# Attention backward on one core: dK's and dV's matmul passes and the V^T transposes moved to other places of a hand-written order

## The chip, the cores and the metric

The kernel runs on one core of one Trainium2 chip. The time is device time in microseconds (us) of one execution. The time before is 5152.12 us, the median of three runs (5147.52 to 5171.49).

## The reference

The reference takes the vector-Jacobian product of a block with attention over a cache and a gated linear unit, and returns the forward output and eight gradients. Cut to what matters here:

```python
xn = layernorm(x)                                # x: 2048 x 576, bf16
q = xn @ wq                                      # 32 heads of 128
scores = einsum("bhqd,bhkd->bhqk", q, k_cache) * 128 ** -0.5
p = softmax(scores)                              # 2048 x 2048 for each head
s = einsum("bhqk,bhkd->bhqd", p, v_cache) @ wo
g = silu((sigmoid(xn @ w_gate) * (xn @ w_up)) @ w_down)
out = x + s * g
# and the gradients of A_x, A_k_cache, A_v_cache, A_wq, A_wo, B_w_gate, B_w_up, B_w_down
```

For each head the backward pass needs S = Q K^T again, P = softmax(S), dP = dO V^T, dS = P (dP - delta), and from them dV = P^T dO, dK = dS^T Q, dQ = dS K, and the output O = P V.

## The kernel before, in words

There are three stages: the feed-forward part (up to about 507 us of the profiled execution), the 32 heads of attention (507 to 3757 us), and the weight gradients and dX (the rest). The change lies in the stage of the heads.

A head has 2048 queries in 16 tiles of 128 and 2048 keys in two halves of 1024. Its work is paced by 64 *halves*. Halves 0 to 31 are the S halves: `s_half` (L457) computes a 128 x 1024 block of S with two matmuls (L465) into one of two PSUM buffers (`ps_big`, two banks each), and VectorE scales it and takes the running row minimum (`sneg`, L467). After both halves of a query tile ScalarE does one exponential over 2048 columns (`s_exp`, L476, `Pq`). Halves 32 to 63 are the dP halves: `dp_half` (L486) does two matmuls (L495) into the same two buffers; VectorE makes dS of the second half directly from PSUM (L498), and for most tiles ScalarE first writes `t` for the first half (L501) and VectorE multiplies it (L505).

All other work of a head fills the room between these pairs of matmuls:

- `rows` and `row_mm` (L525): O from the transposed P (`PT`, with `Vn`) and dQ from the transposed dS (`dST`, with `Kn`), 8 matmuls of 128 columns in every half. The transposes are DMA transposes on SyncE's queue (`trans_dma`, L513), except that of dS tile 9, which TensorE makes.
- `kv` and `kv_mm` (L544): dV from `Pq` and `dOn`, then dK from `dSq` and `Qn`. Each has two passes of 128 matmuls, for one half of the keys each. A pass goes through the 16 query tiles in order, eight matmuls for each, and sums in two PSUM accumulators (`acckv`), which ScalarE then copies out to `kv` (`KVE = "ss"`).
- `proj` (L424, L425): Q^T of the next head and dO^T of this one, in four chunks each, copied out by the engines named in `PJE`.
- `pe_transposes` (L431): K^T, V^T, dO and Q in two groups of eight 128 x 128 transposes; a group goes into one bank and is copied out by the engine named ("v" VectorE, "s" ScalarE, L40 or L42).

GpSimd scales `dOn` by the reciprocal row sums (`s_scale`, L484), two query tiles at a time, after the exponentials and VectorE's reciprocals (L480). `o_sink` copies the O rows (`ou`, ScalarE) and VectorE reduces them to `delta` (L578). `dq_sink` scales dQ on VectorE (`dq_n`, L590).

The four remaining PSUM banks (`ps_acc`, tag "acc") are shared, in turn, by the row accumulators, the dK and dV accumulators, the projections and the transposes. Each new tile takes the bank that has been left longest and waits until its last reader has ended.

The order is written by hand. Every piece of work is put in a list by `at(pos, ...)`, where `pos` counts halves from the head's start (`b`); the list is sorted, and TensorE, VectorE and ScalarE execute their shares in exactly that order. So a position is a place in each engine's queue, not a time. The constants are:

- `VA`, `VB`, `KA`, `KB` (L598): first and last position of dV's two passes and dK's two passes; the 128 matmuls of a pass are spread evenly. Positions from 64 on lie among the S halves of the next head.
- `VT_AT`, `DON_AT` (L600): position of the first group of transposes, distance of the second, and the copying engine.
- `PJE` (L599): copying engine of Q^T's and dO^T's chunks.

Of the kernel before, what the change touches and what calls it, by code (L numbers as in the profile page):

```python
# [95 lines left out]
def kernel(  # L96
# [241 lines left out]
    with tc.tile_pool(name="ld2", bufs=2) as ld2, tc.tile_pool(name="ld1q", bufs=1) as ld1q, \  # L338
# [17 lines left out]
        def at(pos, fn, *args):  # L356
            prog.append((pos, len(prog), fn, args))

        def anchor(pos, fn, *args):
            anchors.append((pos, len(anchors), fn, args))  # L360
# [169 lines left out]
        def rows(pos, step, width, hs, T, rhs, g, sinks):  # L530
            bx = Box()
            sink, after = sinks
            for j in range(GQ):
                for kt in range(NT):
                    at(pos + step * j + width * kt / NT, row_mm, bx, hs, T, rhs, g * GQ + j, kt, sink)
            if after:
                at(pos + step * (GQ - 1) + width + AFTER, after)
# [11 lines left out]
        def kv(pos, end, hs, slabs, rhs, half, out_dram):  # L549
            ov = out_dram.rearrange("(p t) d -> p t d", t=NT)  # L550
            bx = Box()
            bx.acc = [None, None]

            def sink(acc, i):
                c = half * 2 + i
                kv_t = stg.tile([P, KPC, P], bf, name="kv")
                alt.copy(kv_t[:], acc[:], eng=KVE[i])
                nc.gpsimd.dma_start(ov[:, c * KPC:(c + 1) * KPC, :], kv_t[:])

            n = 2 * KPC  # L560
            for qt in range(NT):
                for j in range(n):
                    at(pos + (end - pos) * (qt * n + j) / (NT * n), kv_mm, bx, hs, slabs, rhs, half, qt, j, sink)

        def o_sink(hs, g):
            gs = slice(g * GQ, (g + 1) * GQ)
            bx = Box()

            def sink(acc):
                bx.ou = wt.tile([P, GQ, P], bf, name="ou")  # L570
                alt.copy(bx.ou[:], acc[:], eng=OUE)
                bx.prod = wt.tile([P, GQ, P], f32, name="prod", bufs=1)
                nc.gpsimd.tensor_tensor(bx.prod[:], bx.ou[:], hs.dOn[:, gs, :], op=ALU.mult)

            def after():
                prod, ou = bx.prod, bx.ou
                o_n = stg.tile([P, GQ, P], bf, name="o_n", bufs=1)
                nc.vector.tensor_reduce(hs.delta[:, gs], prod[:], axis=AX.X, op=ALU.add)  # L578
                nc.gpsimd.tensor_scalar(hs.negdelta[:, gs], hs.delta[:, gs], -1.0, None, op0=ALU.mult)  # L579
                nc.gpsimd.tensor_tensor(o_n[:], ou[:], bcast(hs.rinv_all[:, gs], GQ), op=ALU.mult)  # L580
                nc.gpsimd.dma_start(on2_d[g * CH:(g + 1) * CH, hs.h * P:(hs.h + 1) * P].rearrange("(t p) d -> p t d", p=P), o_n[:])

            return sink, after

        def dq_sink(hs, g):
            gs = slice(g * GQ, (g + 1) * GQ)

            def sink(acc):
                dq_n = stg.tile([P, GQ, P], bf, name="dq_n")
                nc.vector.tensor_tensor(dq_n[:], acc[:], bcast(hs.rsc[:, gs], GQ), op=ALU.mult)  # L590
                nc.gpsimd.dma_start(dq2_d[g * CH:(g + 1) * CH, hs.h * P:(hs.h + 1) * P].rearrange("(t p) d -> p t d", p=P), dq_n[:])  # L591

            return sink, None
# [1 line left out]
        H1 = 2 * NT  # L595
        HEAD = 2 * H1
        XO, XQ = 12.1, 12.1
        VA, VB, KA, KB = (22, 38.0), (38.5, 53.5), (58.0, 69.5), (70.5, 82.0)  # L598
        QP, DO, KVE, PJE, OUE = (41.0, 3.0), (4.0, 2.5), "ss", "sv", "s"  # L599
        KT_AT, DON_AT, VT_AT, QN_AT = (46.3, 2, "v"), (7.2, 5, "v"), (22.2, 2, "v"), (38.3, 2, "s")  # L600
        EXP_AT, RINV_AT, PT_AT, DST_AT, AFTER = 2.1, 4.6, 2.7, 2.0, 3.5
        WO_AT = 50.0
        MAN = {mybir.EngineType.PE, mybir.EngineType.DVE, mybir.EngineType.Activation}
        for h in range(H):
            hs = Head(h)
            b = h * HEAD
            back = lambda x: b - HEAD + x if h else b - 14 + x / 8
            at(back(35.0), load_w, hs)
            at(back(35.1), load_kv, hs)
            for c in range(NCH):  # L610
                at(back(QP[0] + QP[1] * c), proj, hs, "QT", c, PJE[0])
                at(b + DO[0] + DO[1] * c, proj, hs, "dOT", c, PJE[1])
            at(b + DO[0] - 2, prep_wo, hs, "s")
            for g in range(2):
                at(back(KT_AT[0] + KT_AT[1] * g), prep_kt, hs, g, KT_AT[2])
                at(b + DON_AT[0] + DON_AT[1] * g, prep_don, hs, g, DON_AT[2])
                at(b + VT_AT[0] + VT_AT[1] * g, prep_vt, hs, g, VT_AT[2])
                at(b + QN_AT[0] + QN_AT[1] * g, prep_qn, hs, g, QN_AT[2])
            for p in range(NT // 2):
                at(b + 4 * p + 2 + RINV_AT, s_rinv, hs, p)  # L620
                at(b + max(4 * p + 2.1 + RINV_AT, DON_AT[0] + DON_AT[1] * (p // 4) + 0.5), s_scale, hs, p)
            for qt in range(NT):
                p1, p2 = b + 2 * qt, b + H1 + 2 * qt
                for hf in range(NHF):
                    anchor(p1 + hf, s_half, hs, qt, hf)
                    anchor(p2 + hf, dp_half, hs, qt, hf)
                at(p1 + EXP_AT, s_exp, hs, qt)
                if qt in PE_P:
                    for g in range(2):
                        at(p1 + 5.3 + g, trans_pe, hs.PT, hs.P, qt, "PT", g, "s")  # L630
                else:
                    at(p1 + PT_AT, trans_dma, hs.PT, hs.P, qt, "PT")
                if qt in PE_DS:
                    for g in range(2):
                        at(p2 + 4.3 + g, trans_pe, hs.dST, hs.dS, qt, "dST", g, "sv"[g])
                else:
                    at(p2 + DST_AT, trans_dma, hs.dST, hs.dS, qt, "dST")
            for g in range(NG):
                rows(b + 8 * g + XO, 2, 2, hs, hs.PT, "Vn", g, o_sink(hs, g))
                rows(b + H1 + 8 * g + XQ, 2, 2, hs, hs.dST, "Kn", g, dq_sink(hs, g))  # L640
            for half, (pv, pk_) in enumerate(((VA, KA), (VB, KB))):
                kv(b + pv[0], b + pv[1], hs, hs.P, "dOn", half, out_3[0, h])
                kv(b + pk_[0], b + pk_[1], hs, hs.dS, "Qn", half, out_2[0, h])
# [380 lines left out]
```

## Time and profile before

| | us |
|---|---|
| median of three runs | 5152.12 |
| profiled execution | 5157.5 |
| its span (first to last instruction) | 5155.7 |
| stage of the 32 heads | about 3250 |
| one head, median of its length | 100.3 |
| TensorE busy in the span | 4983.8 |
| VectorE busy | 3231.5 |
| ScalarE busy | 2285.3 |

The span of the profiled execution is the time from the first to the last instruction; its own time of 5157.5 us includes 1.8 us around that. In the profile PE is TensorE's matmuls, PEld its weight loads, DVE is VectorE, ACT is ScalarE, POOL is GpSimd, SP is SyncE. `out<-in` names what an instruction writes and reads, and L467 is line 467 of the kernel. Matmuls overlap in the records: a matmul of 128 columns is listed with 0.22 us, but they follow each other every 0.0556 us. The granted TensorE clock is 1.00 throughout the heads.

### The profile page before, as it was taken

To read this page: it belongs to the slowest core of one execution; us is meant where nothing else is said; L and a number is where in the kernel's file an instruction comes from. 1 tells how busy PE (TensorE), PEld (TensorE's weight loads), DVE (VectorE), ACT (ScalarE), POOL (GpSimd) and SP (SyncE) were. 2 spreads that over 40 slices of the span, in tenths; PEclk is the share of its full clock that TensorE was granted. 3 is DMA by queue.
4 is the path that set the end of the run, shared out by engine and by line. 5 is a ranking of instruction groups with operands and counts; after the bars stand their busy time and mean duration, and the time that the engine had idled before them with its cause. 6 is when DMAs were issued, how large, how long until landed. Compare 5 with 4: busy or idle time off the path is not lost.

```text
span 5155.7 us, 124622 instructions
## 1 busy us (share of the span) xinstructions
PE 4983.8 (97%) x53232; PEld 3490.9 (68%) x54160; DVE 3231.5 (63%) x5070; ACT 2285.3 (44%) x2878; POOL 1388.1 (27%) x1981
## 2 busy tenths in 40 slices
PE   8999999999999999999999999999899999999999
PEld 3444777777777777777777777777655555554554
DVE  5545888888888888888888888888733222210101
ACT  6531665566556556655655665566501222100000
POOL 2222333233223323332332333233222222111000
PEclk9999999999999999999999999999999999999999
DMA  7478999999999999999999999999999776697775
GB/s 281 184 210 166 189 191 196 195 199 195 196 196 196 197 201 199 196 202 196 199 196 198 199 197 195 199 199 195 205 200 246 209 209 196 199 246 166 158 153 118
DMA packets 2710509, 1013.89 MB, mean 197 GB/s; under 512 B 2523360, under 2 KB 2643936, under 8 KB 2709952
## 3 DMA queue, kind: packets, MB, share of 16 engines
q1 hardware_dynamic: 2628256, 726.57, 81.9%
q0 software_dynamic: 81696, 279.29, 18.5%
q8 instruction: 423, 6.93, 0.5%
q14 instruction: 134, 1.10, 0.1%
HBM read 172.54 MB, written 201.00 MB: 72 GB/s over the span
## 4 chain that ended last, share of the span: by engine, by line
PE 84%; DVE 6%; DMA 5%; issue 4%; SPq 1%; ACT 0%; DVEq 0%; ACTq 0%; another core or an unknown queue 0%
PE acckv L544 17%; PE acc L525 14%; PE acc L965 8%; PE dp L495 6%; PE sp L465 5%; DVE sneg L467 5%; PE accp L424 5%; PE accw L848 5%; DMA dST<-dSq 3%; PE g_ps L249 3%; PE u_ps L252 3%; PE accd L833 3%; PE acc L306 3%; PE acc L903 2%; PE dh L782 2%
## 5 line engine op out<-in xcount | busy, mean ns | idle before, releaser
L476 ACT ACTIVATE Pq<-sneg,nm 128x2048 bf16<-128x2048 bf16 x512 | 1024.5, 2001 | 389.5 <-DVE sneg L467 386.4
L525 PE MATMUL acc<-Kn,dST 128*128 128x128 bf16 x8192 | 1066.6, 219 | 28.1 <-DMA dST<-dSq 26.1
L544 PE MATMUL acckv<-dOn,Pq 128*128 128x128 bf16 x8192 | 1032.1, 219 | 15.4 <-POOL negdelta L579 0.2
L525 PE MATMUL acc<-Vn,PT 128*128 128x128 bf16 x8192 | 1023.2, 219 | 10.9 <-DMA PT<-Pq 9.1
L498 DVE SCALAR_TENSOR_TENSOR dSq<-dp,delta,Pq 128x1024 bf16<-128x1024 f32 x608 | 773.9, 1281 | 351.6 <-PE dp L495 249.7
L544 PE MATMUL acckv<-Qn,dSq 128*128 128x128 bf16 x8192 | 897.7, 220 | 8.4 <-issue 0.2
L544 PEld LDWEIGHTS <-Pq 128*128 128x128 bf16 x8192 | 793.8, 98 | 117.6 <-issue 0.9
L525 PEld LDWEIGHTS <-dST 128*128 128x128 bf16 x8192 | 758.8, 98 | 162.9 <-DMA dST<-dSq 34.1
L525 PEld LDWEIGHTS <-PT 128*128 128x128 bf16 x8192 | 766.4, 98 | 151.2 <-DMA PT<-Pq 11.3
L544 PEld LDWEIGHTS <-dSq 128*128 128x128 bf16 x8192 | 719.7, 98 | 99.8 <-issue 0.3
L467 DVE TENSOR_SCALAR_CACHE_REDUCE sneg<-sp,nm 128x1024 bf16<-128x1024 f32 x512 | 656.5, 1282 | 83.8 <-PE sp L465 46.4
L467 DVE TENSOR_SCALAR_CACHE_REDUCE sneg<-sp 128x1024 bf16<-128x1024 f32 x512 | 625.1, 1221 | 60.4 <-PE sp L465 42.0
L501 ACT ACTIVATE t<-dp,negdelta 128x1024 bf16<-128x1024 f32 x416 | 463.6, 1114 | 425.7 <-PE acc L525 233.2
L465 PE MATMUL sp<-KT,QT 128*128 128x512 bf16 x1763 | 548.4, 380 | 33.0 <-DVE sneg L467 26.1
L495 PE MATMUL dp<-VT,dOT 128*128 128x512 bf16 x1728 | 540.4, 379 | 0.8 <-DVE dSq L498 0.8
L484 POOL TENSOR_TENSOR dOn<-dOn,rinv_all 128x256 bf16<-128x256 bf16 x256 | 155.9, 609 | 657.7 <-DVE rinv_all L480 540.6
L505 DVE TENSOR_TENSOR dSq<-t,Pq 128x1024 bf16<-128x1024 bf16 x416 | 319.5, 768 | 0.0
L848 PE MATMUL accw<-dd_blk,xn_all 128*128 128x512 bf16 x1134 | 250.6, 379 | 0.9
L978 DVE SCALAR_TENSOR_TENSOR junk<-dxn,xn_all 128x576 f32<-128x576 f32 x16 | 12.1, 758 | 368.2 <-ACT dxn L973 368.2
L965 PEld LDWEIGHTS <-cf 128*128 128x128 bf16 x2304 | 145.7, 98 | 142.7 <-DMA cf<-dg_d 4.5
L591 POOL DMA_DIRECT2D dq_d<-dq_n x128 | 98.7, 771 | 459.5 <-DVE dq_n L590 450.9
L848 PEld LDWEIGHTS <-xn_all 128*128 128x128 bf16 x1152 | 111.4, 98 | 133.8
(182 smaller groups left out, 6694.3 us busy)
## 6 DMA issues: line engine op xcount, KB each, us to landing
out_dram<-kv POOLq DMA_DIRECT2D x256, 128.0 KB, 5.2
h_d<-h_row POOLq DMA_DIRECT2D x48, 384.0 KB, 2.7
a_d<-a_row POOLq DMA_DIRECT2D x48, 384.0 KB, 2.6
b_d<-b_row POOLq DMA_DIRECT2D x48, 384.0 KB, 3.2
a_blk<-a_d SPq DMA_DIRECT2D x18, 1024.0 KB, 5.6
b_blk<-b_d SPq DMA_DIRECT2D x18, 1024.0 KB, 20.8
du_d<-dd_blk POOLq DMA_DIRECT2D x18, 1024.0 KB, 8.5
dg_d<-dd_blk POOLq DMA_DIRECT2D x18, 1024.0 KB, 11.5
```

The lines of the kernel that those rows point to most:

```text
L424: nc.tensor.matmul(acc[:], lhsT=w[:, i, :], rhs=srcT[:, i, cs], start=(i == 0), stop=False)
L465: nc.tensor.matmul(sp[:, c * CH:(c + 1) * CH], lhsT=hs.QT[:, qs], rhs=hs.KT[:, hf * HW_ + c * CH: hf * HW_ + (c + 1) * CH], start=True, st ...
L467: nc.vector.tensor_scalar(sneg[:, hf * HW_:(hf + 1) * HW_], sp[:], -SCALE, None if hf == 0 else nm[:, hf - 1:hf], op0=ALU.mult, op1=ALU.mi ...
L476: nc.scalar.activation(Pq[:], sneg[:], AF.Exp, bias=nm[:, hf:hf + 1], scale=-1.0, accum_out=hs.rs_all[:, qt:qt + 1])
L495: nc.tensor.matmul(dp[:, c * CH:(c + 1) * CH], lhsT=hs.dOT[:, qs], rhs=hs.VT[:, hf * HW_ + c * CH: hf * HW_ + (c + 1) * CH], start=True, s ...
L498: nc.vector.scalar_tensor_tensor(dSq[:, hsl], dp[:], hs.delta[:, qt:qt + 1], Pq[:, hsl], op0=ALU.subtract, op1=ALU.mult)
L501: nc.scalar.activation(t[:], dp[:], AF.Identity, bias=hs.negdelta[:, qt:qt + 1], scale=1.0)
L505: nc.vector.tensor_tensor(dSq[:, hsl], t[:], Pq[:, hsl], op=ALU.mult)
L525: nc.tensor.matmul(bx.acc[:, j, :], lhsT=T[qt][:, kt, :], rhs=getattr(hs, rhs)[:, kt, :], start=(kt == 0), stop=(kt == NT - 1))
L544: nc.tensor.matmul(bx.acc[i][:, jj, :], lhsT=slabs[qt][:, k0:k0 + P], rhs=getattr(hs, rhs)[:, qt, :], start=(qt == 0 and jj == 0), stop=(q ...
L848: nc.tensor.matmul(acc[:], lhsT=xn_all[:, st, i * P:(i + 1) * P], rhs=dd_blk[:, st, :, :], start=(st == 0), stop=(st == NT - 1))
L965: nc.tensor.matmul(accs[sl][j][:, :nn], lhsT=ch[:, kk, sl * P:(sl + 1) * P], rhs=w_[:, n0:n0 + nn], start=(pi == 0 and kk == 0), stop=(las ...
```

## The change

Three lines of constants and the two places that read one of them are changed. dV's first pass begins 0.7 halves earlier and ends 0.6 earlier, its second is spread over 16.1 instead of 15 halves. dK's first pass begins 1.5 halves later and ends 1.1 later, its second begins 0.6 later and ends 2.9 later, at 84.9, which is half 20.9 of the next head. The second group of dO's transposes comes one half later. V^T's two groups stand at 22.6 and 26.6 instead of 22.2 and 24.2, and ScalarE copies them. The third chunk of dO^T is copied by ScalarE instead of VectorE. The number of instructions on each engine's path is otherwise the same.

```diff
-        VA, VB, KA, KB = (22, 38.0), (38.5, 53.5), (58.0, 69.5), (70.5, 82.0)
-        QP, DO, KVE, PJE, OUE = (41.0, 3.0), (4.0, 2.5), "ss", "sv", "s"
-        KT_AT, DON_AT, VT_AT, QN_AT = (46.3, 2, "v"), (7.2, 5, "v"), (22.2, 2, "v"), (38.3, 2, "s")
+        VA, VB, KA, KB = (21.3, 37.4), (37.9, 54.0), (59.5, 70.6), (71.1, 84.9)
+        QP, DO, KVE, PJE, OUE = (41.0, 3.0), (4.0, 2.5), "ss", ("ssss", "vvsv"), "s"
+        KT_AT, DON_AT, VT_AT, QN_AT = (46.3, 2, "v"), (7.2, 6, "v"), (22.6, 4, "s"), (38.3, 2, "s")
...
-                at(back(QP[0] + QP[1] * c), proj, hs, "QT", c, PJE[0])
-                at(b + DO[0] + DO[1] * c, proj, hs, "dOT", c, PJE[1])
+                at(back(QP[0] + QP[1] * c), proj, hs, "QT", c, PJE[0][c])
+                at(b + DO[0] + DO[1] * c, proj, hs, "dOT", c, PJE[1][c])
```

## The prediction

> **What bounds the kernel now.** I read the page first (engine shares, chain), then the chain of waits in one head, then the timelines of ScalarE and VectorE there.
>
> ```profile
> PE 4983.8 (97%) x53232; PEld 3490.9 (68%) x54160; DVE 3231.5 (63%) x5070; ACT 2285.3 (44%) x2878; POOL 1388.1 (27%) x1981
> PE 84%; DVE 6%; DMA 5%; issue 4%; SPq 1%; ACT 0%; DVEq 0%; ACTq 0%; another core or an unknown queue 0%
> ```
>
> TensorE is the bound: only what leaves it idle in a head can be won, 32 times over. The chain, in order of time (start, length, what), shows where VectorE takes it from TensorE:
>
> ```profile
> 2457.85 0.45 PE sp L465 x2
> 2458.34 0.07 issue
> 2458.41 1.23 DVE sneg L467 x2
> 2459.64 0.09 DVE rinv_all L480
> 2459.77 0.58 DVE sneg L467
> 2460.35 0.63 issue
> 2460.98 1.24 DVE sneg L467 x3
> ...
> 2464.77 0.06 DVE VT L42
> ...
> 2470.09 0.09 DVE sneg L467
> 2470.23 0.38 PE sp L465
> ```
>
> Numbering a head's halves 0 to 63 (S halves 0 to 31, dP halves from 32), 2457.6 is the start of half 18 of this head. From the starts of the weight loads of L465 and L495 a head takes 100.3 us (median). Its TensorE work, from the same chain, is 0.43 for a half's two 512-column matmuls, 0.0556 for each 128-column matmul (0.45 for eight) and 1.08 for a projection: 97.9 us. Half by half, length minus work is almost everywhere 0.00 to 0.01 us. The exceptions:
>
> - half 12: 0.39. The second transpose group of dO^T wants the bank that dq_n (L590) still empties.
> - halves 20, 21, 22: 0.25, 0.54, 0.27. Halves 18 to 21 hold 0.88 us of matmuls, while VectorE's two sneg take 2.56 per pair (2458.41 to 2460.98).
> - half 27: 0.46. VectorE is still behind by two V^T copies and one delta.
> - half 41: 0.16 (a Qn copy), half 58: 0.09 (the t of half 56).
>
> Together 2.16 us a head. Some heads lose 1 to 2 us more at halves 56 to 60, where dST arrives late.
>
> **The change, part by part.** The built order shows that nothing is added or removed on TensorE; 289 matmuls of dK and dV in the S halves replace 269. Halves 18 to 21 go from 0.88 to 1.38, 1.38, 1.32 and 1.21 us, V^T's groups go from halves 22 and 24 to 22 and 26, dO^T's second group from 12 to 13; halves 58 and 59 fall from 1.54 and 1.49 to 0.88 and 1.21.
>
> *Gains.* Halves 20 to 22: the work now exceeds VectorE's 1.28 a half, so 1.06 goes. Half 27: VectorE loses two copies of 0.69, so 0.46 goes; the delta left at half 23 delays sneg by 0.6, inside the lead of two score buffers. Half 12: dq_n ended 1.0 after the half's start (2448.84 against 2447.84); the group now starts 1.9 after it, so 0.39 goes. Sum 1.91. The dO^T copy (0.69 on VectorE, 0.585 as ScalarE's QT row) hides behind half 10 on either engine.
>
> *Costs.* Each stretch of dK or dV needs two of the four accumulator banks, and ScalarE empties the old ones between softmax exponentials of 2.0 us:
>
> ```profile
> 2457.48 1.07 ACT L40 CAST kv<-acckv 128x512 bf16<-128x512 f32 x2 [0.22 <-ACT Pq L476]
> 2458.44 2.02 ACT L476 ACTIVATE Pq<-sneg,nm 128x2048 bf16<-128x2048 bf16 x1
> 2460.34 0.20 ACT L476 ACTIVATION_READ_ACCUMULATOR Pq<-sneg,nm 128x1 f32 x1
> 2460.43 0.58 ACT L40 CAST ou<-acc 128x512 bf16<-128x512 f32 x1
> 2461.09 2.00 ACT L476 ACTIVATE Pq<-sneg,nm 128x2048 bf16<-128x2048 bf16 x1
> ```
>
> Before, dK's last copies had four halves before dV wanted the banks. Now dK ends at 20.9 and dV starts at 21.3; ScalarE's order there becomes exp 8, ou, exp 9, the two dK copies, exp 10. The build makes dV's second accumulator (half 21, eleventh filler) wait for the first dK copy.
>
> *Half 21.* Count from half 17's start. Halves 17 to 20 take 1.44, 1.38, 1.39, 1.32, so half 20 starts at 4.21 and half 21 at 5.53. ou starts 0.31 after half 20 (as 2482.40 against a half start of 2482.09) and holds ScalarE 0.49: until 5.01. exp 9 could go at 4.83, so ou ends last; it runs to 7.00. First dK copy: 7.00 to 7.58 (0.58); TensorE follows an ending copy by 0.05 (2490.10 to 2490.15). The matmul could have run at 5.53 + 0.06 + 0.43 + 10 x 0.0556 = 6.58. Wait 1.05. Behind it in TensorE's queue stands half 22, so all stands.
>
> *Half 28.* The dK copies end ScalarE's work at 7.95, exp 10 at 9.94, V^T copy 1 (1.0, as the Qn copy's 1.018) at 10.94. Half 22 starts at 7.85, half 24 at 10.95; delta puts its sneg at 12.11 and the next at 13.46, so exp 12 runs from 14.79 to 16.78 and V^T copy 2 to 17.80. Half 28 starts at 16.70; its new row accumulator takes that bank and could start at 17.25: wait 0.60. Nothing waits for V^T itself so early, only for the bank.
>
> *Half 7.* dK's first half ends at 6.6, so exp 2 is now ahead of its copies. From half 5: exp 2 from 2.02 to 4.01, copy to 4.59; the second half's first matmul could start at 4.39: wait 0.25.
>
> *Half 59.* Half 58 without dK lasts 0.88; half 59 needs the buffer that VectorE reads from 2516.62 to 2517.90. It could start 0.88 after 2516.76, at 2517.64: wait 0.31. dST of tile 8 is reached 0.5 us sooner; its landing had 1.2 us to spare (median), so nothing more in most heads.
>
> *Half 35.* dV's tile 14 moves from half 36 to 35.4; POOL's scaling ends 4.74 after half 32 and the matmul could start at 4.76: 0.05.
>
> *Elsewhere.* 0.16 and 0.09 stay; half 40 is one matmul shorter and its Qn group one matmul later: 0.11 more at half 41. exp 15 starts 1.76 after half 32 as before (2478.55), so PT transposes on SP keep their lead of 2 to 9 us. POOL stores dK one to three halves later, in time it had idle.
>
> The Trainium skill, "PSUM — Partial Sum Buffer", section "Engine vs sequencer instructions", says that ScalarE's queue is a strict FIFO: a copy can't pass an exponential. The first row above, a copy released by the end of an exponential, agrees; if a copy could pass, the wait at half 21 would be nothing.
>
> The Trainium skill, "ScalarE: Activation LUTs", section "Rules for kernel authors", sends simple elementwise work to VectorE as up to three times faster in bf16, which speaks against moving the V^T copies. The rows say 1.018 against 0.686 us; kept on VectorE they would cost the 0.46 of half 27 and save the 0.60 of half 28, 4 us less in all.
>
> **The sum.** After: 0.25 + 1.05 + 0.60 + 0.05 + 0.27 + 0.09 + 0.31 = 2.62 us a head; before 2.16. The 0.46 more, times 31, is 14 us. Head 0 has no dK ahead of it and gains about 1.5 (an estimate from 1.06 + 0.46); behind the last head 15 more matmuls stand alone, 0.8 us. Net 14 us. The profiled execution was 5157.5 us (span 5155.7), 5.4 above the median 5152.1; I add to the median: 5166. What this measurement can tell from no change is about 0.5%, 26 us or 0.8 us a head.
>
> **Rivals.** *The fillers work (faster).* ScalarE is free in time at halves 21 and 28: 1.05 and 0.60 vanish, 1.19 us a head is won, 37 us: 5115. For: ScalarE is busy only 44%. Against: its order, and 2.0 us exponentials just ahead of the copies. It decides if the first dK copy ends by 6.5 on the scale above.
>
> *dST arrives late (slower).* With dK gone from halves 58 and 59, tile 8's rows lose 0.5 us of cover. For, from the view of waits (us, times, longest):
>
> ```profile
> PE acc L525 <- DMA dST<-dSq: 26.1, 24, 6.5
> ```
>
> In 8 of 32 heads tile 8 landed with no time to spare. Against: the median has 1.2 us to spare. If landings come 0.7 later, from transposes running closer together, 0.8 us a head is added on top of the forecast: 14 + 25, 5191. From a landing 0.7 us later than now it decides.
>
> *The change doesn't do what it says*: the built order has the matmuls in halves 18 to 21, so no.
>
> **How the numbers follow.** Forecast 0.53, faster rival 0.17, slower 0.30. The forecast's own range is 5140 to 5182 (half 28 between 0 and 1.2, half 21 between 0.8 and 1.3, half 59 between 0 and 0.5 us). Of its 0.53, 0.48 lies within 0.5% and 0.05 above; 0.02 of the slower rival stays within, and 0.01 of the faster one. So faster 0.16, same 0.51, slower 0.33. The range reaches to both rivals: 5112 to 5195.
>
> **What would show it.** Right: in TensorE's waits a new group, acckv L544 or the halves behind it held by ScalarE's kv copies at half 21, about 1 us in every head; no idle at halves 12, 20 and 27; a head of about 100.8 us. V^T rows on ScalarE with about 1.02 us each, exp 12 ahead of the second. Wrong: halves 21 and 28 at their matmul time (then the faster rival), or dST in the waits at half 60 well above 26 us (the slower one).

## The result: 0.4% slower, and the profile after

The changed kernel takes 5179.42 us (median of 21 runs, 5164.31 to 5206.34); the kernel before, run beside it, 5161.39 (21 runs, 5144.1 to 5193.11). The ratio is 1.0037, with a 95% interval of 1.0023 to 1.0051: 18 us slower by the medians, 19 by the ratio. Forecast were 5166 against 5152.12, 14 us slower. Its profiled execution took 5182.66 us, its span 5180.8.

The page of the changed kernel, engine shares and chain:

```profile
PE 4979.2 (96%) x53263; PEld 3493.4 (67%) x54160; DVE 3187.1 (62%) x4974; ACT 2349.9 (45%) x2974; POOL 1386.3 (27%) x1981
PE 82%; DMA 5%; DVE 5%; issue 4%; ACT 4%; SPq 0%; ACTq 0%; DVEq 0%; another core or an unknown queue 0%
```

TensorE's share of the chain falls from 84 to 82%. ScalarE, at 0% before, now has 4% of it. TensorE's waits in the changed kernel (us in total, times, longest) say where:

```profile
PE acckv L544 <- ACT kv L40: 32.7, 62, 0.9
PE acc L525 <- DMA dST<-dSq: 31.6, 20, 5.1
PE acc L525 <- ACT VT L40: 13.3, 30, 0.6
...
PE sp L465 <- DVE sneg L467: 7.9, 12, 1.8
...
PE dp L495 <- DVE dSq L498: 3.8, 20, 0.9
```

The first and third rows are new: the dK and dV accumulators wait for ScalarE's copies twice in each of 31 heads, and the rows of O wait for the V^T copy once in each of 30. In exchange, the waits for VectorE's sneg have fallen from 26.1 us to 7.9, and those of the dO^T group for dq_n are gone. The chain of the changed kernel, in the same head as before, shows halves 21 and 28 (start, length, what):

```profile
2471.55 0.39 ACT Pq L476
2472.02 1.09 issue
2473.11 0.19 ACT Pq L476
2473.30 0.48 ACT kv L40
2473.82 0.22 PE acckv L544
...
2480.93 2.09 ACT Pq L476 x2
2483.03 0.91 ACT VT L40
2483.98 0.22 PE acc L525
```

Both times the chain runs through an exponential, the copy queued behind it on ScalarE, and the matmul that wanted the bank. (Its "issue" of 1.09 lies inside the exponential, as the timeline of ScalarE there shows.)

```profile
2471.20 2.00 ACT L476 ACTIVATE Pq<-sneg,nm 128x2048 bf16<-128x2048 bf16 x1
2473.11 0.19 ACT L476 ACTIVATION_READ_ACCUMULATOR Pq<-sneg,nm 128x1 f32 x1
2473.20 1.06 ACT L40 CAST kv<-acckv 128x512 bf16<-128x512 f32 x2
```

Two lengths of a head are used from here on, both from the starts of the weight loads, with heads counted from 0. The *mean head* is the mean length of heads 1 to 30: 101.87 us against 100.97 before the change. The *undisturbed head* takes for each of the 64 halves the median of its length over heads 2 to 30 and adds these up: 100.91 us against 100.32. Waits that come in less than half of the heads are in the first and not in the second. The idle time of TensorE by half, median, in us:

| half | 7 | 12 | 20 | 21 | 22 | 27 | 28 | 35 | 41 | 58 | 59 | 62 |
|---|---|---|---|---|---|---|---|---|---|---|---|---|
| before | 0.01 | 0.39 | 0.25 | 0.54 | 0.27 | 0.46 | 0 | 0 | 0.16 | 0.09 | 0.01 | 0 |
| forecast | 0.25 | 0 | 0 | 1.05 | 0 | 0 | 0.60 | 0.05 | 0.27 | 0.09 | 0.31 | 0 |
| after | 0.39 | 0 | 0 | 0.99 | 0.01 | 0 | 0.60 | 0.05 | 0.22 | 0.09 | 0.32 | 0.11 |

### The profile page after: what moved, and what is told of

Its sections match the earlier page's. It is cut to its first block, busy times and chain, and to the rows that moved or that the text cites. A ratio compares the mean times of both kernels' runs of the same rounds, so it can differ in the third digit from the quotient of the medians.

```text
span 5180.8 us, 124624 instructions
## 1 busy us (share of the span) xinstructions
PE 4979.2 (96%) x53263; PEld 3493.4 (67%) x54160; DVE 3187.1 (62%) x4974; ACT 2349.9 (45%) x2974; POOL 1386.3 (27%) x1981
## 3 DMA queue, kind: packets, MB, share of 16 engines
q14 instruction: 133, 1.09, 0.1%
## 4 chain that ended last, share of the span: by engine, by line
PE 82%; DMA 5%; DVE 5%; issue 4%; ACT 4%; SPq 0%; ACTq 0%; DVEq 0%; another core or an unknown queue 0%
PE acckv L544 16%; PE acc L525 14%; PE acc L965 7%; PE dp L495 6%; PE sp L465 5%; PE accw L848 5%; PE accp L424 4%; DVE sneg L467 3%; PE u_ps L252 3%; PE g_ps L249 3%; PE accd L833 3%; PE acc L306 3%; DMA dST<-dSq 3%; PE acct L431 3%; PE acc L903 2%
## 5 line engine op out<-in xcount | busy, mean ns | idle before, releaser
L544 PE MATMUL acckv<-dOn,Pq 128*128 128x128 bf16 x8192 | 1066.5, 219 | 34.3 <-ACT kv L40 25.7
L525 PE MATMUL acc<-Kn,dST 128*128 128x128 bf16 x8192 | 1052.9, 220 | 34.9 <-DMA dST<-dSq 31.6
L525 PE MATMUL acc<-Vn,PT 128*128 128x128 bf16 x8192 | 1049.5, 219 | 23.2 <-ACT VT L40 13.3
L498 DVE SCALAR_TENSOR_TENSOR dSq<-dp,delta,Pq 128x1024 bf16<-128x1024 f32 x608 | 773.9, 1281 | 347.5 <-PE dp L495 320.4
L544 PE MATMUL acckv<-Qn,dSq 128*128 128x128 bf16 x8192 | 923.0, 220 | 18.6 <-ACT kv L40 7.0
L525 PEld LDWEIGHTS <-PT 128*128 128x128 bf16 x8192 | 791.6, 98 | 165.0 <-issue 29.8
L544 PEld LDWEIGHTS <-dSq 128*128 128x128 bf16 x8192 | 732.3, 98 | 99.6 <-issue 0.6
L591 POOL DMA_DIRECT2D dq_d<-dq_n x128 | 98.6, 771 | 446.2 <-DVE dq_n L590 433.4
```

The costliest lines, as they stand in the source:

```text
L498: nc.vector.scalar_tensor_tensor(dSq[:, hsl], dp[:], hs.delta[:, qt:qt + 1], Pq[:, hsl], op0=ALU.subtract, op1=ALU.mult)
L525: nc.tensor.matmul(bx.acc[:, j, :], lhsT=T[qt][:, kt, :], rhs=getattr(hs, rhs)[:, kt, :], start=(kt == 0), stop=(kt == NT - 1))
L544: nc.tensor.matmul(bx.acc[i][:, jj, :], lhsT=slabs[qt][:, k0:k0 + P], rhs=getattr(hs, rhs)[:, qt, :], start=(qt == 0 and jj == 0), stop=(q ...
```

## Experiments

Two theories about the time stood against each other. **A**, the one that the prediction's sum rests on: a head lasts as long as TensorE's matmuls and its regular waits, so each wait taken away is won 31 times. **B**: the 31 DMA transposes of a head are already near what their queue can do, and TensorE time that is won comes back as waits for them. The table has all kernels; "DMA" is the number of transposes that a head sends to the DMA queue, "waits" is TensorE's waits for dST and PT together, and a ratio is to the kernel before on the same chip. Of the waits, 13 to 23 us lie in the last head of every kernel (20.9 of the 35.2 before, 13.9 of the 39.6 after). The undisturbed and the mean head come from the one profiled execution of each kernel; the expectations below say "median head" for the undisturbed one. The plain median of the heads' lengths is another number, for it contains the irregular waits: 100.8 us in f_all_banks_free, 103.4 and 103.7 in the two kernels with 32.

| kernel | DMA | undisturbed head | mean head | waits | ratio to before, 95% interval |
|---|---|---|---|---|---|
| before | 31 | 100.32 | 100.97 | 35.2 | 1 |
| after | 31 | 100.91 | 101.87 | 39.6 | 1.0037 [1.0023, 1.0051] |
| e_copies_before_exp9 | 31 | 100.24 | 101.18 | 45.4 | 1.0031 [1.0008, 1.0053] |
| e_vt_by_vector | 31 | 100.32 | 101.05 | 38.8 | 1.0036 [1.0015, 1.0057] |
| e_dk_first_back | 31 | 100.22 | 102.16 | 67.6 | 1.004 [1.0019, 1.006] |
| e_before_don6 | 31 | 99.95 | 101.39 | 51.6 | 0.9991 [0.9971, 1.0011] |
| f_all_banks_free | 31 | 99.34 | 101.21 | 66.0 | 1.0003 [0.9987, 1.0018] |
| f_all_tile7_pe | 31 | 99.62 | 101.60 | 73.3 | 1.0028 [1.0012, 1.0045] |
| f_after_tile7_pe | 31 | 101.17 | 101.70 | 34.4 | 1.0041 [1.0023, 1.0059] |
| f_before_don6_tile7_pe | 31 | 100.10 | 101.16 | 40.7 | 0.9992 [0.9976, 1.0009] |
| g_before_no_pe_tile | 32 | 100.61 | 103.81 | 117.4 | 1.018 [1.0156, 1.0204] |
| g_all_no_pe_tile | 32 | 99.33 | 103.90 | 161.5 | 1.0187 [1.0165, 1.0209] |
| g_all_pt14_pe | 30 | 100.89 | 100.91 | 12.8 | 0.998 [0.9965, 0.9995] |
| i_all_ds10_pe | 30 | 99.84 | 100.23 | 22.8 | 0.9929 [0.9904, 0.9954] |

### One term at a time

**Half 21: dK's end in front of exponential 9** (the changed kernel, with dK's second pass 0.9 halves shorter):

```diff
-        VA, VB, KA, KB = (21.3, 37.4), (37.9, 54.0), (59.5, 70.6), (71.1, 84.9)
+        VA, VB, KA, KB = (21.3, 37.4), (37.9, 54.0), (59.5, 70.6), (71.1, 84.0)
```

> The changed kernel, with dK's second pass ending at 84.0 instead of 84.9, so that ScalarE's two dK copies come before exp 9 in its order; dV still begins at 21.3. Theory (the bank waits behind one exponential): the idle of half 21 falls from 0.99 to 0.1 us or less, half 28 keeps about 0.6, a head takes 100.0 instead of 100.9 us, the kernel is about 28 us faster than the changed one (0.5%). Rival (ScalarE has too much to do between halves 18 and 28, whatever the order): the wait of half 21 is only moved, halves 28 and 35 grow by what 21 loses, a head stays at 100.6 us or more.

Half 21's idle went from 0.99 to 0.00, half 28's from 0.60 to 0.85, and the undisturbed head to 100.24. The wait at half 21 is therefore the copy behind that exponential. The time did not follow: it stayed 0.3% over before, where 28 us less than the changed kernel were expected.

**Half 28: the V^T copies on VectorE again**, still four halves apart:

```diff
-... VT_AT, QN_AT = ... (22.6, 4, "s"), (38.3, 2, "s")
+... VT_AT, QN_AT = ... (22.6, 4, "v"), (38.3, 2, "s")
```

> The changed kernel, with V^T's copies by VectorE again, at the new places 22.6 and 26.6. Theory (half 28 waits for the bank of ScalarE's second V^T copy): half 28 falls from 0.60 to nearly nothing, VectorE's lag gives 0.05 to 0.25 us at halves 25 to 28, 0.35 us a head or 11 us in all is won. Rival (VectorE then lags as in the kernel before): 0.46 us or more of idle appears at halves 25 to 28, and 4 us or nothing is won.

Half 28's 0.60 went, and half 27 stayed at 0.00: with four halves between them, VectorE carries both copies without falling behind at half 27, at least as long as half 21 still waits its 0.99. The prediction had charged 0.46 for that. The undisturbed head is before's again, 100.32, and still the ratio is 1.0036. (The profiled execution of this kernel, 5163 us, was the fastest of its 12; their median is 5184. So its mean head of 101.05 is too short for a typical one.)

**Halves 7, 59 and 62: dK's first pass where it was:**

```diff
-        ... (59.5, 70.6), (71.1, 84.9)
+        ... (58.0, 69.5), (71.1, 84.9)
```

> The changed kernel, with dK's first pass at 58.0 to 69.5 as before (the second stays at 71.1 to 84.9). Theory (ScalarE's copies behind exp 2 cost half 7, the uncovered halves 58 and 59 cost 59, 60 and 62): 0.39, 0.32 and 0.11 go, and the mean of half 60 falls from 0.36 to about 0.16: 0.8 us a head in the median, 1.0 in the mean, 25 to 31 us in all. Rival (the later dST landings come from the whole order's closer spacing, not from these halves): half 60 keeps its mean of 0.36, and about 0.8 us a head are won.

The three waits went and the undisturbed head fell by 0.69 us, but the mean rose to 102.16: waits for dST are 52.2 us and for PT 15.4, where the changed kernel had 31.6 and 8.0.

**Half 12: only dO^T's second group one half later**, in the kernel before:

```diff
-        ... DON_AT ... = (7.2, 5, "v")
+        ... DON_AT ... = (7.2, 6, "v")
```

> The kernel before, with the second group of dO^T's transposes one half later (13.2 instead of 12.2), nothing else. Theory: only half 12's 0.39 us goes, a head takes 99.9 instead of 100.3 us, 12 us less than before (0.24%). Rival (the stall moves to half 13 or to the O rows that start there): no change.

Half 12's 0.39 went and the undisturbed head fell by 0.37, while the waits for DMA rose by 16 us. No difference in time can be told.

### The waits for ScalarE's copies away at once, and another tile for TensorE

**The waits of halves 7, 21, 28, 59 and 62 taken away** (the changed kernel, with dV's first pass and both of dK's moved, and V^T on VectorE):

```diff
-        VA, VB, KA, KB = (21.3, 37.4), (37.9, 54.0), (59.5, 70.6), (71.1, 84.9)
+        VA, VB, KA, KB = (20.9, 37.4), (37.9, 54.0), (58.0, 69.5), (70.5, 84.0)
...
-... VT_AT, QN_AT = ... (22.6, 4, "s"), (38.3, 2, "s")
+... VT_AT, QN_AT = ... (22.6, 4, "v"), (38.3, 2, "s")
```

> The changed kernel with every wait that its profile shows taken away by its place: dV from 20.9, dK's first pass back at 58.0 to 69.5, the second at 70.5 to 84.0 (its copies ahead of exp 9), V^T's copies by VectorE at 22.6 and 26.6. Theory A (the waits of halves 7, 21, 28 and 59 are what the change lost): a median head of about 98.6 us with 0.5 us of idle, and the time follows: 1.7 us a head or about 50 us less than the kernel before (1%). Theory B (the transposes by DMA land too late for a shorter head): the median head is 98.6 us as well, but TensorE's waits for dST and PT grow from 35 us by 20 to 50 us, and the kernel wins less than 0.5% or nothing.

The undisturbed head is 99.34, 1.57 less than in the changed kernel and 0.98 less than before. It did not come down to the expected 98.6: half 26 has a new wait of 0.34 for VectorE's sneg, behind the first V^T copy and a delta, half 58 waits 0.40, mostly for dST, and halves 41 and 35 keep 0.22 and 0.16. By A 0.98 us a head is 30 us faster than before; measured is 1.0003. Its waits:

```profile
PE acc L525 <- DMA dST<-dSq: 47.6, 37, 5.6
PE acc L525 <- DMA PT<-Pq: 18.4, 20, 5.7
PE sp L465 <- DVE sneg L467: 11.3, 40, 1.0
```

The gain is there in an undisturbed head and is taken back in irregular waits for the transposes. Half 58, where dST is waited for most, is where TensorE begins the rows of tile 7, and half 60 where it begins those of tile 8. Three kernels gave TensorE dS's tile 7 in place of tile 9:

```diff
-    PE_DS = {9}
+    PE_DS = {7}
...
-                        at(p2 + 4.3 + g, trans_pe, hs.dST, hs.dS, qt, "dST", g, "sv"[g])
+                        at(p2 + 7.3 + 2 * g, trans_pe, hs.dST, hs.dS, qt, "dST", g, "sv"[g])
```

In f_all_banks_free:

> The kernel of the run before, with dS tile 7 transposed by TensorE in place of tile 9 (at 53.3 and 55.3), so that tile 9 goes by DMA, where the built order leaves it ten halves. Nothing else: the same number of transposes by each. Theory B: the waits for dST at half 58 vanish and those at 60 shrink, 0.4 to 0.8 us a head or 12 to 25 us less than the run before. Theory A: no difference (within 0.2%).

In the changed kernel:

> The changed kernel, with dS tile 7 transposed by TensorE in place of tile 9. Theory B: the mean excess of half 58 (0.31 us over the median head) goes, half 60 keeps part of its 0.34; 10 to 15 us less than the changed kernel, while halves 7, 21 and 28 keep 0.39, 0.99 and 0.60. Theory A: no difference.

In e_before_don6:

> The kernel before, with the second dO^T group one half later and dS tile 7 transposed by TensorE in place of tile 9. Theory B: half 12's 0.39 and half 58's mean of 0.4 to 0.7 us are gone, 0.8 us a head or 25 us less than the kernel before (0.5%). Theory A: 12 us less (0.24%).

Half 58's mean idle fell to 0.07 us in all three, and half 60's below 0.1, so the lateness of tiles 7 and 8 can be cured there. The time that B expected from it, 10 to 25 us, did not come; the lateness comes back elsewhere. The waits of f_all_tile7_pe:

```profile
PE acc L525 <- DMA PT<-Pq: 48.0, 50, 3.8
PE acc L525 <- DMA dST<-dSq: 25.3, 19, 6.7
```

Together they are 7.3 us more than without the move: dST's have halved, and P's late tiles at halves 34 and 36 have taken their place. None of the three became faster.

### Changing the number of DMA transposes

**One more in the kernel before** (32 by DMA, 0.89 us less on TensorE):

```diff
-    PE_DS = {9}
+    PE_DS = set()
```

> The kernel before, with dS's tile 9 transposed by the DMA queue like the other fifteen, so that 32 transposes a head go by DMA and none by TensorE; TensorE's matmuls of a head fall from 97.86 to 96.97 us. Theory A (TensorE's work and its regular waits set the time of a head): 0.89 us less on each of 31 heads, 28 us or 0.5% faster than before. Theory B (the DMA queue's transposes, 31 to a head, are near their limit, and time won on TensorE comes back as waits for them): TensorE's waits for DMA, some 35 us in the trace of before, grow by 28 us or more; the time is the kernel before's within 0.3%, or longer.

**The same in f_all_banks_free:**

> The kernel of f_all_banks_free, with dS's tile 9 transposed by DMA too: 32 transposes a head by DMA. Theory A: a median head of 98.5 us and 28 us faster than f_all_banks_free. Theory B: the median head falls, but the mean head stays between 101 and 102.5 us, TensorE's waits for DMA pass 90 us, and the time is f_all_banks_free's or longer.

Both are 1.8 to 1.9% slower than before, with less work on TensorE: A had the sign wrong. B had the sign but not the size: it expected "within 0.3%, or longer", and heads of up to 102.5 us where 103.8 and 103.9 were found. The waits of g_before_no_pe_tile:

```profile
PE acc L525 <- DMA dST<-dSq: 80.4, 61, 5.9
PE acc L525 <- DMA PT<-Pq: 37.0, 47, 3.1
```

Two kernels whose undisturbed heads differ by 1.28 us have mean heads within 0.1 us of each other. Divided by 32, 103.81 and 103.90 give 3.24 and 3.25 us for one transpose: here the DMA transposes, one after another, and not TensorE, set the head. Times 31 that is 100.6 us, and no kernel with 31 transposes in the table has a mean head below 100.97.

**One fewer**, f_all_banks_free with P's tile 14 by TensorE and VectorE:

```diff
-    PE_P = set()
+    PE_P = {14}
...
-                        at(p1 + 5.3 + g, trans_pe, hs.PT, hs.P, qt, "PT", g, "s")
+                        at(p1 + 5.3 + g, trans_pe, hs.PT, hs.P, qt, "PT", g, "v")
```

> The kernel of f_all_banks_free, with P's tile 14 transposed by TensorE and copied by VectorE, so that 30 transposes a head go by DMA and two tiles by TensorE; TensorE's matmuls of a head grow by some 0.9 us. Theory A: 31 x 0.9 = 28 us slower than f_all_banks_free, a median head of 100.2 us. Theory B: TensorE's waits for DMA, 66 us in f_all_banks_free, fall by half or more, and the mean head comes to within 0.7 us of the median head; the time is f_all_banks_free's within 0.3% or shorter.

Mean and undisturbed head are the same to 0.02 us. In heads 0 to 30 no wait for DMA remains; the two below lie in the last head:

```profile
PE acct L431 <- DVE PT L42: 18.5, 32, 0.6
PE sp L465 <- DVE sneg L467: 11.2, 42, 1.0
...
PE acc L525 <- DMA dST<-dSq: 7.0, 1, 7.0
...
PE acc L525 <- DMA PT<-Pq: 5.8, 1, 5.8
```

TensorE has 0.89 us more work a head than in f_all_banks_free, and a new wait of 0.6 for VectorE's copy, and the kernel is not slower for it (0.998 against 1.0003). The undisturbed head is 0.7 us above the 100.2 of A's sum, most of it that new wait; the mean, which sets the time, is below f_all_banks_free's.

**One fewer, in a better place**: dS's tile 10 instead, in halves 56 and 57, where a half has only 0.88 us of work:

```diff
-    PE_DS = {9}
+    PE_DS = {9, 10}
```

> The kernel of f_all_banks_free, with dS's tile 10 transposed by TensorE beside its tile 9 (halves 56 and 57, where a half is shortest and two acc banks are free), so that 30 transposes a head go by DMA and P's all do. Theory B, with the limit read from the two kernels of 32 transposes (103.8 us a head, 3.24 us for each): 30 transposes need 97.3 us, below TensorE's own time, so the mean head comes down to the median, that is 99.34 us + 0.89 us of transposes, less 0.3 us of half 58's wait: 100.0 us, 31 x (101.0 - 100.0) = 30 us or 0.6% faster than before. Theory A (TensorE's sum alone): 28 us slower than f_all_banks_free, 0.5% slower than before.

```profile
PE acc L525 <- DMA dST<-dSq: 17.2, 14, 3.9
PE sp L465 <- DVE sneg L467: 13.0, 42, 1.8
...
PE acc L525 <- DMA PT<-Pq: 5.6, 1, 5.6
```

It takes 5135.36 us against 5168.24 for the kernel before on the same chip: 0.9929 [0.9904, 0.9954], 33 us by the medians or 0.7% by the ratio faster than before, where B forecast 30 us and A 0.5% slower, and the fastest of all. The mean head, 100.23 where B expected 100.0, is 0.98 below f_all_banks_free's, although TensorE does more, and 0.74 below before's.

## Why the prediction was right, and where it was not

**The order of work.** Every wait that was to go went (halves 12, 20 to 22, 27), and every one that was to come came. Half 21: exponential 9 was to start 5.01 us after half 17 (at 2466.27) and started 4.93 after it; the matmul that the copy releases was to run at 7.63 and ran at 7.55. Half 28 came to 0.60 as forecast. The idle sum of a head, 2.62 by the forecast, is 2.78 by the table; the undisturbed head grew by 0.59 us against 0.46. Head 0 fell by 1.2 us (96.27 to 95.04) for the 1.5 estimated.

**What was mis-sized.** *Half 7*: 0.39 for 0.25. The exponential ran as reckoned (2447.09 to 2449.09), but the copy started 0.11 after its end and not at it. *Half 62*: 0.11 that the prediction did not have: in the heads that show it, VectorE's dS of half 60 (L498) ends 0.11 us after half 62's first weight load. (The last row of the waits above, also for VectorE's dS, is half 59's, which came out at 0.32 for 0.31.) *Half 41*: 0.22 for 0.27. *V^T on VectorE*: the step that charged 0.46 at half 27 for keeping the copies there did not hold. In e_vt_by_vector it cost nothing; with half 21's wait gone too, in f_all_banks_free, it comes with 0.34 at half 26.

**The rivals.** That the fillers work is refuted by halves 21 and 28. That dST arrives late came in part: its waits rose from 26.1 to 31.6 us, and half 60's mean idle from 0.16 to 0.36 us, a quarter of the price of 0.8 a head. Tile 8's landing, which had 1.2 us to spare by the median, had 0.3 left, where the prediction took off 0.5. Tile 7, which it does not name, had as little: 1.1 us before, 0.6 after.

**What the sum left out.** The step from idle time to time is not borne out. The prediction took TensorE for the only bound ("only what leaves it idle in a head can be won") and multiplied the idle time of an undisturbed head by 31. For the 0.59 us found that gives 18 us, as measured. But when the added waits were taken away again, the time did not come back: e_vt_by_vector and e_copies_before_exp9 have before's undisturbed head and are still 0.3% slower than before, and f_all_banks_free has 0.98 us less and is no faster. In the two profiled executions the mean head grew by 0.90 us and not by 0.59, because irregular waits rose too. So the place and size of the new waits are shown, but not that the 0.4% is made of them: that the sum came out so close is in part luck.

The number of DMA transposes moves the time at once, in both directions. The prediction read the dST row as a risk to one tile; it was the sign of a second bound, level with TensorE: 31 x 3.24 = 100.6 us against an undisturbed head of 100.32.

The trace of before could have told a part of it: of the 992 transposes in its heads, 2 were issued with none in flight, 703 with one and 287 with two. The mean busy share of the DMA queue could not: between 1000 and 3500 us it is 100.6% before, and 100.0% in i_all_ds10_pe, which is faster. SyncE's own row tells more. Its issuing instruction of a transpose (L513) lasts 3.0 us by the median, and the next one starts 0.1 us after it. So a tile that is ready can stand in line: from the end of a P tile's exponential to the start of its transpose's issue pass 1.5 us before the change, 2.0 after it, 2.9 in f_all_banks_free, 5.0 and 5.5 in the kernels with 32, and 0.4 to 0.5 in those with 30 (medians of heads 1 to 30).

The Trainium skill, "DMA: Bandwidth & Descriptors", section "Latency and other measured facts", gives DMA transposes 261 GB/s, measured on one kernel, and more where data is contiguous. A transpose here moves 128 x 2048 values of 2 bytes, 0.524 MB; in 3.24 us that is 162 GB/s, beside 33 GB/s of GpSimd's queue, so the measurement disagrees. As an estimate from the page's figure, a transpose would take 2.0 us and 32 of them 64 us of a head's 101: far too little to make the two kernels with 32 slower.

**Open.** What makes the changed kernel 0.4% slower is not settled. Five kernels with 31 transposes that were made from it lie at 1.003 to 1.004 and f_all_banks_free at 1.0003, the two made from before at 0.999, and one profiled execution of each has mean heads of 101.0 to 102.2 us in no clear order. Late exponentials that leave the DMA queue with nothing to do would be one reason, but the traces do not bear it out: SyncE's pauses of over 0.2 us before a transpose add up to 2.2 us a head before the change and to 1.1 after it. What limits a transpose to 3.24 us was not tried either: the DMA queue may hold SyncE's issuing instruction up, or that instruction may be the limit itself.

## What to carry to other kernels

When TensorE's regular waits are removed and the time stays, compare the mean of a repeated stage with its undisturbed length, the sum of the medians of its parts: a gap between them that grows as the undisturbed length falls hints at a second bound. The median of the whole stage can hide it: in the kernels with 32 transposes it lies within 0.4 us of the mean, while the undisturbed head is 3.2 and 4.6 us below. Test it by changing the number of its operations by one in both directions, not only by moving them. Where a queue and an engine are level, a piece of work moved from the queue to the engine pays even though the engine has the larger busy share, if it lies where the engine has room.

## What the runs showed of the hardware

- A transpose of 128 x 2048 bf16 from SyncE's queue takes 5.7 to 6.3 us from the start of its issue to landing (medians of P's and dS's in before and after), but in the kernels with 32 a head one is done every 3.24 us, and in before and after never were more than two others in flight at an issue. The issuing instruction itself lasts 3.0 us on SyncE (median; 1.3 at the shortest). One more a head, 32 for 31, cost 2.7 to 2.8 us of the mean head.
- A PSUM copy of ScalarE released TensorE within 0.05 us of its end (2473.78 to 2473.82 and 2483.94 to 2483.98 in the chain above), so the place of a copy in ScalarE's queue is nearly all of such a wait.
